# A linear-attention normalizer replicated over the partitions: TensorE matmuls exchanged for a round trip through DRAM

## Chip, cores and metric

The kernel runs on one core of a Trainium2 chip. The metric is the device time of one execution in microseconds; the time before is the median of three runs. A profile was taken of one further execution. Engines are named as in the profile: PE is TensorE (PEld its weight loads), DVE VectorE, ACT ScalarE, POOL GpSimd, SP SyncE, which issues most DMAs here.

## What is computed

A token block of 2048 x 640 is layer-normalized; one branch is a linear attention with 32 heads of width 20 and a learned feature map, the other a gated MLP of width 1536; their product is added to the input. Cut to what matters here:

```python
qkv = (xn @ wqkv)                            # q, k, v: 32 heads of width 20
pq, pk = q @ w_phi, k @ w_phi                # per head
phi_q = concat(softmax(pq), softmax(-pq))    # 40 features per head
phi_k = concat(softmax(pk), softmax(-pk))
kv  = einsum("bhsf,bhsd->bhfd", phi_k, v)
z   = einsum("bhsf->bhf", phi_k)             # the normalizer: 32 * 40 = 1280 numbers
num = einsum("bhqf,bhfd->bhqd", phi_q, kv)
den = einsum("bhqf,bhf->bhq", phi_q, z) + 1e-6
s   = (num / den) @ wo
g   = silu(gelu(xn @ w1 + b1) @ w2 + b2)
out = x + s * g
```

The change concerns `z` alone: 1280 numbers that must stand on all 128 partitions, because queries lie with one token on each partition and `den` is formed there by an elementwise product and sums.

## The kernel before

**Phase 1 (to about 249 us)** goes over 16 tiles of 128 tokens: keys, values and queries are projected on TensorE in three passes of split floats (`project`, L332), exponentials are formed, and key-value products are accumulated in one PSUM bank named `kv` (`kv_acc`, L403), two tiles of tokens in one go. A value tile carries a column of ones beside each head, so one row of each head's block of `kv` is the sum of its key features, which is `z`. Exponentials of the queries are stored to DRAM (`e_dram`). At the end of the phase `kv_rest` copies the bank to the SBUF tile `kvr` (128 x 360) by three ScalarE copies (L607): the normalizer then lies in four rows of `kvr`, on partitions 20, 52, 84 and 116, as pieces of 120 numbers (three heads each).

**Phase 2 (to about 535 us)** is the MLP, in 12 units: two halves of the tokens by 6 groups of 256 hidden columns. Its instructions are put out in the order written by hand. A unit runs, on TensorE, the seven parts of the hidden layer (`part`, L654, 54 matmuls of 512 columns, a scheme of sums and differences that saves products), then two down-projections (`down`, L683, 30 matmuls each). Around them:

- ScalarE applies Gelu (`act`, L659) and forms the high half of a hidden tile (L661), VectorE the low half (`act_lo`, L665). The tiles are named h11, h22, h21, h12 in the order of their making; the first down-projection uses h11 and h21, the second h12 and h22. VectorE collects the down-projections (L690 in the first group, L692 later).
- The next unit's `w1` forms are made on GpSimd (L419) and split by ScalarE (L430) and GpSimd (L431); `w2` is split by ScalarE (L146) and GpSimd (L148; VectorE in unit 0).
- SP's queue gets, in each unit and in this order, the raw weight loads of the next unit (L154), a block of normalized inputs (`xhi`, `xlo`, L703 and L704) and the exponentials of a block of queries (`eq`, L723).
- `q_norm` normalizes that block of queries: GpSimd multiplies it with the replicated normalizer (`ez<-eq,zrep`, L729), VectorE sums over heads, GpSimd scales (L371), and SP stores the result to `phi_dram` (L746).

In unit 0, between the last part of the hidden layer and the first down-projection, stands the call

```python
        if unit == 0:
            zf = kv_norm(kvr)
```

`kv_norm` makes the replicated normalizer `zrep` (128 x 1280, in one of 23 rotating slabs). Its first reader is `q_norm` of the query block that unit 1 treats; its last is near the end of the kernel. PSUM is a pool of eight banks (`bankB`) by then, given out in rotation.

**Phase 3 (from about 535 us)** forms the attention's numerators (L773, L784), projects with `wo` (L848), applies the gate and stores.

A pattern of the change is in the kernel already: `pair_stats` stores means and scales of two tiles to `st_dram` (L293) and loads them back broadcast over all partitions (L295).

The functions that the change touches, with the line numbers of the profile:

Of the kernel before, what the change touches and what calls it, by code (L numbers as in the profile page):

```python
# [8 lines left out]
F32 = mybir.dt.float32  # L9
F32R = mybir.dt.float32r  # L10
AF = mybir.ActivationFunctionType
# [3 lines left out]
S, D, H, DH, F = 2048, 640, 32, 20, 1536  # L15
P = 128
# [30 lines left out]
def hedgehog_gated_mlp_kernel(ctx: ExitStack, tc: tile.TileContext, x, xt_in, wqk, bd, wv, wo, w1, b1, w2, b2, out_t):  # L47
    nc = tc.nc
# [4 lines left out]
    dram = ctx.enter_context(tc.tile_pool(name="dram", bufs=1, space=bass.MemoryType.DRAM))  # L53
# [27 lines left out]
    def slab(dt, name, shape=(P, 2, D)):  # L81
        return slabs.tile(list(shape), dt, tag="S", name=name)
# [7 lines left out]
    def bankB(name="pB"):  # L90
        return pools["B"].tile([P, 512], F32, tag="B", name=name)
# [4 lines left out]
    xd_dram = dram.tile([P, 9, 2, CW], F32, name="xd_dram")  # L96
    w1_dram = dram.tile([NG, P, 2, 2048], F32, name="w1_dram")
    g_dram = dram.tile([KC, P, 2, CW], F32, name="g_dram")
    st_dram = dram.tile([NT // 2, 2, P, 2], F32, name="st_dram")

    ident = const.tile([P, P], F32, name="ident")
# [499 lines left out]
    def kv_rest():  # L601
        kv_pair(NT - 2)
        kvr = const.tile([P, 360], F32, name="kvr")
        nc.gpsimd.memset(kvr[64:96, 320:360], 0.0)
        nc.gpsimd.memset(kvr[96:, 240:360], 0.0)
        for p, a, b in ((P, 0, 240), (96, 240, 320), (64, 320, 360)):
            nc.scalar.activation(kvr[:p, a:b], kvp[0][:p, a:b], AF.Copy)  # L607
        return kvr


    def kv_state(kvr):
# [8 lines left out]
        for r in range(3):  # L620
            nc.vector.tensor_tensor(bdl[:80, 40 * r:40 * r + 40].rearrange("p (h d) -> p h d", d=20),
                                    ps[:80, None, 320:340].to_broadcast([80, 2, 20]),
                                    mask[:80, :2, None].to_broadcast([80, 2, 20]), op=OP.mult)
    def kv_norm(kvr):
        zf = slab(F32, "zrep")[:].rearrange("p a b -> p (a b)")
        for e, n in enumerate((360, 360, 320, 240)):
            ps = bankB()
            nc.tensor.matmul(ps[:, :n], ident[:, 32 * e + 20:32 * e + 21].to_broadcast([P, P]), kvr[:, :n],
                             start=True, stop=True)
            m = n // 120  # L630
            nc.scalar.activation(zf[:, :960].rearrange("p (g r) -> p g r", r=480)[:, :, 120 * e:120 * e + 120],
                                 ps[:, :240].rearrange("p (g r) -> p g r", r=120), AF.Copy)
            if n > 240:
                nc.scalar.activation(zf[:, 960 + 120 * e:720 + 120 * e + n], ps[:, 240:n], AF.Copy)
        return zf


# [220 lines left out]
    zf, none = None, iter(())  # L858
# [6 lines left out]
    kvr = kv_rest()  # L865
# [8 lines left out]
    for unit in range(units):  # L874
        h, g = divmod(unit, NG)
# [69 lines left out]
        if unit == 0:  # L945
            zf = kv_norm(kvr)
# [146 lines left out]
```

## Time and profile before

| | |
|---|---|
| median of three runs | 681.69 us (680.76, 681.69, 681.69) |
| the profiled execution | 680.42 us, of which the span of the instructions 678.7 us |
| PE busy | 673.7 us, 99% of the span |
| PEld busy | 591.3 us, 87% |
| DVE busy | 456.4 us, 67% |
| POOL busy | 382.1 us, 56% |
| ACT busy | 253.1 us, 37% |
| granted TensorE clock | full in all 40 slices |
| DMA | 125.42 MB, in the mean 185 GB/s |

The page gives busy shares over the span. A busy share is an average, and a matmul's recorded end is modelled; what an instruction costs is read from start to start in the timeline, and whether it matters from the chain that ended last and from the view of waits. A line number in the profile is that of the kernel before; a helper's line stands for all its calls.

### The profile page before, as it was taken

Reading aid. Unit: us, or ns where it says so; the run is one execution under the profiler, and the core shown is the slowest. Engines: PE = TensorE matmul, PEld = TensorE weight load, DVE = VectorE, ACT = ScalarE, POOL = GpSimd, SP = SyncE. Lnnn points to the kernel's source line nnn. Section 1 sums busy time; section 2 is a strip of 40 time slices with the busy share of each in tenths; the row PEclk is TensorE's granted clock in tenths of the full one; section 3 lists DMA queues with packets and bytes.
Section 4 is the critical chain, followed back from the end, with each engine's and each line's share of the span. In section 5 each row is a group of like instructions: output and inputs, shape, how many; then the busy total and the mean of one; then the engine's idle time right before and its main releaser. Section 6 shows DMA issues by size and latency. Waiting matters only on the chain.

```text
span 678.7 us, 11993 instructions
## 1 busy us (share of the span) xinstructions
PE 673.7 (99%) x4727; PEld 591.3 (87%) x4727; DVE 456.4 (67%) x729; ACT 253.1 (37%) x400; POOL 382.1 (56%) x351
## 2 busy tenths in 40 slices
PE   9999999999999999999999999999999999999998
PEld 9999999999999998888888888888888887777877
DVE  5786575887786456586988784586876665774232
ACT  3523213333223237244245238533133264425440
POOL 3653355757668275857878861716546640783221
PEclk9999999999999999999999999999999999999999
DMA  8820234543441433339678696477363491988433
GB/s 335 309 79 2 32 121 125 203 108 122 96 174 59 158 123 117 110 111 359 205 248 307 242 427 249 148 247 256 125 216 116 178 384 35 330 292 286 154 93 109
DMA packets 73966, 125.42 MB, mean 185 GB/s; under 512 B 5822, under 2 KB 42686, under 8 KB 73014
## 3 DMA queue, kind: packets, MB, share of 16 engines
q1 hardware_dynamic: 71606, 114.17, 49.0%
q10 hardware_dynamic: 2304, 10.49, 4.2%
q8 instruction: 37, 0.61, 0.4%
q14 instruction: 19, 0.16, 0.1%
HBM read 79.54 MB, written 45.10 MB: 184 GB/s over the span
## 4 chain that ended last, share of the span: by engine, by line
PE 93%; DMA 3%; DVE 2%; POOL 1%; issue 1%; SPq 0%; ACT 0%; DVEq 0%; POOLq 0%
PE pA L332 30%; PE pB L683 23%; PE pB L654 20%; PE pB L848 11%; PE pB L784 3%; PE kv L403 2%; PE pB L773 2%; DMA raw<-in_wo_dram 2%; DMA phi<-phi_dram 1%; PE pA L173 1%; POOL wv L148 1%; PE pA L470 1%; PE pA L318 1%; PE pB L791 1%; DVE st L197 0%
## 5 line engine op out<-in xcount | busy, mean ns | idle before, releaser
L683 PE MATMUL pB<-hs,w2s 128*128 128x512 f32 x720 | 167.1, 390 | 0.0
L683 PEld LDWEIGHTS pB<-hs,w2s 128*128 128x128 f32 x720 | 134.7, 188 | 29.3 <-PE pB L784 0.8
L654 PE MATMUL pB<-xp,w1s 128*128 128x512 f32 x324 | 81.3, 389 | 0.0
L654 PE MATMUL pB<-xd,w1s 128*128 128x512 f32 x324 | 79.3, 389 | 0.0
L358 ACT ACTIVATE e<-e 128x1280 f32<-128x1280 f32 x32 | 40.7, 1273 | 92.2 <-POOL e L353 91.8
L848 PE MATMUL pB<-oT,wo 128*128 128x512 f32 (+2 forms) x315 | 73.9, 386 | 0.0
L692 DVE TENSOR_TENSOR y<-pB,y 128x512 f32<-128x512 f32 x100 | 63.8, 679 | 12.3 <-PE pB L683 12.1
L654 PEld LDWEIGHTS pB<-xd,w1s 128*128 128x128 f32 x324 | 60.8, 188 | 12.6
L654 PEld LDWEIGHTS pB<-xp,w1s 128*128 128x128 f32 x324 | 60.7, 188 | 12.7 <-DVE pB L929 0.2
L848 PEld LDWEIGHTS pB<-oT,wo 128*128 128x128 f32 x315 | 57.1, 188 | 14.2 <-ACT ph L776 1.2
L371 POOL TENSOR_TENSOR eq<-eq,rc 128x1280 f32<-128x1280 f32 x16 | 37.9, 2370 | 50.8 <-DVE rc L742 50.8
L371 POOL TENSOR_TENSOR e<-e,rc 128x1280 f32<-128x1280 f32 x16 | 39.0, 2439 | 47.4 <-DVE rc L391 47.1
L353 POOL TENSOR_TENSOR e<-nr,e 128x640 f32<-128x640 f32 x32 | 45.5, 1424 | 29.9 <-DVE nr L352 26.6
L332 PE MATMUL pA<-wv,xp 128*128 128x320 f32 x384 | 60.5, 310 | 0.3 <-POOL wv L148 0.3
L659 ACT ACTIVATE pB<-pB,b1t 128x512 f32<-128x512 f32 x48 | 31.8, 662 | 75.7 <-PE pB L654 26.7
L332 PE MATMUL pA<-wk,xp 128*128 128x320 f32 x384 | 59.6, 310 | 0.0
L332 PE MATMUL pA<-wq,xp 128*128 128x320 f32 x384 | 58.8, 309 | 0.0
L332 PEld LDWEIGHTS pA<-wv,xp 128*128 128x128 f32 x384 | 57.0, 188 | 0.5 <-POOL wv L148 0.5
L332 PEld LDWEIGHTS pA<-wq,xp 128*128 128x128 f32 x384 | 56.9, 188 | 0.3 <-PE pA L332 0.3
L332 PEld LDWEIGHTS pA<-wk,xp 128*128 128x128 f32 x384 | 56.9, 188 | 0.0
L729 POOL TENSOR_TENSOR ez<-eq,zrep 128x1280 f32<-128x1280 f32 x16 | 47.3, 2958 | 0.4 <-PE pB L784 0.2
L431 POOL TENSOR_TENSOR w1s<-raw,w1s 128x640 fp32r<-128x640 f32 (+1 forms) x18 | 25.7, 1427 | 37.0 <-ACT w1s L430 29.9
(145 smaller groups left out, 1052.6 us busy)
## 6 DMA issues: line engine op xcount, KB each, us to landing
raw<-in_w_dram SPq DMA_DIRECT2D x42, 320.0 KB, 4.3
e_dram<-e ACTq DMA_DIRECT2D x16, 640.0 KB, 3.2
eq<-e_dram SPq DMA_DIRECT2D x16, 640.0 KB, 6.8
phi_dram<-eq SPq DMA_DIRECT2D x16, 640.0 KB, 3.5
phi<-phi_dram SPq DMA_DIRECT2D x16, 640.0 KB, 8.7
xt<-in_x_dram SPq DMA_DIRECT2D x16, 320.0 KB, 5.2
xres<-in_xt_dram SPq DMA_DIRECT2D x20, 256.0 KB, 4.2
out_dram<-xres SPq DMA_DIRECT2D x18, 256.0 KB, 3.0
```

The source lines that it names most:

```text
L332: nc.tensor.matmul(ps[:, hf, :HALF], stat_x(q, o, k, a), ws[k][:, b, hf * HALF:(hf + 1) * HALF], start=n == 0, stop=n == 3 * KC - 1)
L353: nc.gpsimd.tensor_tensor(e5[:, :, :, 1, :], nr[:, :, :, None].to_broadcast([P, 2, 16, DH]), e5[:, :, :, 0, :], op=OP.subtract)
L358: nc.scalar.activation(ef, ef, AF.Exp)
L371: nc.gpsimd.tensor_tensor(e3, e3, rc[:, :, None].to_broadcast([P, 64, DH]), op=OP.mult)
L431: nc.gpsimd.tensor_tensor(sl[:, 1, :n], src, sl[:, 0, :n].bitcast(F32), op=OP.subtract)
L654: nc.tensor.matmul(bank[ch][:], tl[:, a, off + wo_:off + wo_ + P], mov(blk, b), start=new and n == 0, stop=n == len(mms) - 1, skip_group_c ...
L659: nc.scalar.activation(ps, ps, AF.Gelu_apprx_tanh, bias=b1t[:, f:f + 1])
L683: nc.tensor.matmul(ps[:], ws[i][:, b, d * P:(d + 1) * P], hs[o][i][:, a, :], start=i == n == 0, stop=(i, n) == (GF - 1, 2), skip_group_che ...
L692: nc.vector.tensor_tensor(y, ps[:], y, op=OP.add)
L729: nc.gpsimd.tensor_tensor(zv, ef, zf, op=OP.mult)
L784: nc.tensor.matmul(po[64 * e:64 * e + 64, :256], bdk[:n, 2 * j + e, :], ph[:n, e * 256:(e + 1) * 256], start=True, stop=True)
L848: nc.tensor.matmul(ps[:, mv], w, o[:, mv], start=n == 0, stop=n == 15, skip_group_check=True)
```

## The change

In `kv_norm`, four matmuls go that each replicated one row of `kvr` over the partitions (a column of the identity matrix, repeated 128 times, as the weights), with four PSUM banks and the seven ScalarE copies that took the pieces to their places in `zrep`. In their stead five small DMAs store the pieces of the four rows in the right order to a DRAM tensor `z_dram`, and one DMA loads its first 1280 numbers to all 128 partitions. All six are issued by SP, at the same place in the order of the calls. `q_norm` and the rest are as before.

```diff
+    z_dram = dram.tile([1440], F32, name="z_dram")
...
     def kv_norm(kvr):
+        zv = z_dram.rearrange("(g e r) -> e g r", e=4, r=120)
+        for e, m in enumerate((3, 3, 2, 2)):
+            nc.sync.dma_start(zv[e:e + 1, :m], kvr[32 * e + 20:32 * e + 21, :120 * m].rearrange("p (g r) -> p g r", r=120))
+        nc.sync.dma_start(z_dram[1200:2 * D].unsqueeze(0), kvr[84:85, 240:320])
         zf = slab(F32, "zrep")[:].rearrange("p a b -> p (a b)")
-        for e, n in enumerate((360, 360, 320, 240)):
-            ps = bankB()
-            nc.tensor.matmul(ps[:, :n], ident[:, 32 * e + 20:32 * e + 21].to_broadcast([P, P]), kvr[:, :n],
-                             start=True, stop=True)
-            m = n // 120
-            nc.scalar.activation(zf[:, :960].rearrange("p (g r) -> p g r", r=480)[:, :, 120 * e:120 * e + 120],
-                                 ps[:, :240].rearrange("p (g r) -> p g r", r=120), AF.Copy)
-            if n > 240:
-                nc.scalar.activation(zf[:, 960 + 120 * e:720 + 120 * e + n], ps[:, 240:n], AF.Copy)
+        nc.sync.dma_start(zf, z_dram[:2 * D].partition_broadcast(P))
         return zf
```

In the built order of instructions TensorE has the four matmuls less, ScalarE the seven copies less, and SP the six DMAs more: after the load of the exponentials for unit 1 and before the raw weight loads for unit 2. VectorE and GpSimd have the same instructions in the same order.

## The prediction

> **What bounds the kernel now.** I read the page first, and in it the shares of the chain that ended last.
>
> ```profile
> PE 93%; DMA 3%; DVE 2%; POOL 1%; issue 1%; SPq 0%; ACT 0%; DVEq 0%; POOLq 0%
> ```
>
> TensorE (PE) carries 93% of the chain. Next I asked the view of waits for TensorE alone; this is all of it (engine and line that waited, who released it, us in total, times, longest):
>
> ```profile
> PE pA L470 <- PEq L1083: 0.8, 1, 0.8
> PE pA L332 <- POOL wv L148: 0.3, 1, 0.3
> PE pB L784 <- DVE oT L788: 0.3, 1, 0.3
> PE pA L318 <- DVE xt L213: 0.2, 1, 0.2
> ```
>
> TensorE waits 1.6 us in the whole run. So its instruction stream is the clock of this kernel: what is taken out of that stream shortens the run by its length, unless something then comes late. Third, the chain in order of time around the change (start, us, what):
>
> ```profile
> 261.29 2.15 PE pB L628 x8
> 263.45 13.63 PE pB L683 x60
> 277.08 12.24 PE pB L654 x54
> 289.32 13.60 PE pB L683 x60
> ```
>
> The four normalizer matmuls (L628; eight records) lie on the chain between unit 0's hidden-layer matmuls (L654) and its first down-projection (L683). In unit 1 L683 follows L654 with nothing between: what unit 0 will look like afterwards.
>
> **The change, part by part.**
>
> *TensorE's four matmuls go.* The timeline of TensorE alone (start, us, engine, line):
>
> ```profile
> 259.09 2.20 PE L654 MATMUL pB<-xp,w1s 128*128 128x512 f32 x9
> 261.13 2.31 PE L628 MATMUL pB<-kvr,ident 128*128 128x360 f32 x8
> 263.11 8.08 PE L683 MATMUL pB<-hs,w2s 128*128 128x512 f32 x34
> ```
>
> Three readings of their price: start to start, 263.11 − 261.13 = 1.98 us; the chain's piece, 2.15; the busy time with the modelled end of the last, 2.31. I take 1.98: ends are modelled, starts are recorded, and the neighbour before them also hands over from start to start (261.13 − 259.09 = 2.04 for nine matmuls). Ends for the range: 1.98 to 2.31, less what comes late instead.
>
> The Trainium skill, "TensorE: Matmul & The Clock Gate" (Part 1: The HAM clock gate), has back-to-back matmuls of N columns start N ÷ 2.4 GHz + about 2.5 ns apart. By that rule eight records of 320 columns in the mean would take some 1.1 us (an estimate from the page), the gain would be 1.1 us and the time 680.6; the starts above do not agree, at 248 ns each.
>
> *What is late next on TensorE.* The down-projection would begin at 261.13. It goes through nine matmuls on h11 and then to h21; one matmul takes 13.60/60 = 0.227 us by the chain's row. The halves of h11 and h21 come from ScalarE (ACT, the high half) and VectorE (DVE, the low half). Two timelines, of DVE and of ACT:
>
> ```profile
> 260.11 0.69 DVE L665 TENSOR_TENSOR hs<-pB,hs 128x512 fp32r<-128x512 f32 x1
> 261.29 0.69 DVE L665 TENSOR_TENSOR hs<-pB,hs 128x512 fp32r<-128x512 f32 x1 [0.49 <-ACT hs L661]
> 262.48 0.69 DVE L665 TENSOR_TENSOR hs<-pB,hs 128x512 fp32r<-128x512 f32 x1 [0.49 <-ACT hs L661]
> ```
>
> ```profile
> 261.85 0.60 ACT L661 ACTIVATE hs<-pB 128x512 fp32r<-128x512 f32 x1
> ...
> 264.50 0.60 ACT L661 ACTIVATE hs<-pB 128x512 fp32r<-128x512 f32 x1
> ...
> 266.41 0.81 ACT L430 ACTIVATE w1s<-raw 128x640 fp32r<-128x640 f32 x1
> ```
>
> The three DVE rows are the low halves of h11, h22 and h21. None of these instructions depends on the removed matmuls, so they keep their times. h11's low half is done at 260.80 and needed at the third matmul, 261.13 + 2 × 0.227 = 261.58. h21's high half is done at 262.45 and needed at the tenth, 263.17; its low half is done at 263.17 and needed at the twelfth, 263.63. The narrowest margin is 0.46 us. If it fails, TensorE loses what is missing, tenths at most. h12's high half ends at 265.10, its low half 0.69 later, for the second down-projection at 261.13 + 30 × 0.227 = 267.9. Accumulator banks: four fewer are drawn, so the down-projections take over banks from the hidden layer's parts, as they do in every later unit.
>
> *Seven ScalarE copies go* (L631, L634). They stand between 265.10 and the next unit's weight copies (L430) at 266.41, so L430 moves up by 1.31 us, and with it GpSimd's (POOL's) halves of those weights. ScalarE is not on the chain here: no gain of its own, but the weights of unit 1 keep pace with a TensorE that arrives 1.98 earlier, except for 0.67 us.
>
> *Six DMAs come on SP's queue*, after the load of query block 8 (L723) and ahead of the four weight loads for unit 2 (L154). SP's own timeline, and the ScalarE row that finishes `kvr`:
>
> ```profile
> 232.62 0.73 SPq L704 DMA_DIRECT2D xlo<-xp_dram  x1
> 233.46 1.84 SPq L723 DMA_DIRECT2D eq<-e_dram  x1
> 245.20 11.64 SPq L154 DMA_DIRECT2D raw<-in_w_dram  x4
> 269.63 0.53 SPq L703 DMA_DIRECT2D xhi<-xp_dram  x1
> ```
>
> ```profile
> 249.58 0.55 ACT L607 ACTIVATE kvr<-kv 128x240 f32<-128x240 f32 x3
> ```
>
> The kernel has the same pattern already: layer-norm statistics are stored to DRAM and loaded back broadcast over partitions. Its rows price the new one, with the longest of its own size beside them: the DMA issues (last column: median us to landing), and the issue itself on SP (ns, the least, median and most).
>
> ```profile
> eq<-e_dram SPq DMA_DIRECT2D x16, 640.0 KB, 6.8
> ...
> bc<-st_dram SPq DMA_DIRECT2D x4, 256.0 KB, 5.6
> ...
> st_dram<-pst SPq DMA_DIRECT2D x4, 2.0 KB, 2.8
> ```
>
> ```profile
> L293 SPq DMA_DIRECT2D st_dram<-pst x4: 359/360/367, 76.5 to 176.3; - x4
> ```
>
> `kvr` is complete at 250.13. Five stores at 0.36 are issued by 251.9; the last lands 2.8 later (a store of 2 KB) or at worst 6.8 (640 KB), 254.7 to 258.7; the spread, 640 KB, is issued in another 0.36 and lands 5.6 to 6.8 later: 260.7 to 265.9. I take the early end, since the stores hold 5 KB together. Its slab's last reader is the final query projection, long past. Who waits for it is GpSimd's first `ez` (L729):
>
> ```profile
> 276.87 2.96 POOL L729 TENSOR_TENSOR ez<-eq,zrep 128x1280 f32<-128x1280 f32 x1
> 279.79 3.10 POOL L148 TENSOR_TENSOR w2s<-raw,w2s 128x640 fp32r<-128x640 f32 x2
> 285.32 0.74 POOL L419 TENSOR_TENSOR st<-raw 128x256 f32<-128x256 f32 x1 [2.44 <-PE pB L654]
> ```
>
> Even 1.98 earlier, `ez` starts at 274.9, 9 us after the latest landing. Behind `ez` on GpSimd stand unit 1's `w2s` halves; the first is needed at the second matmul of unit 1's down-projection, 289.32 + 0.23 − 1.98 = 287.6, so `ez` may start as late as 287.6 − 1.55 − 2.96 = 283.1. Against that the spread has 17 us of cover or more.
>
> Queued behind the spread's wait are the four raw loads. The first, at 245.20 before, now goes out at 255.1 to 259.1; even with 6.8 to land it is there by 266, and its first user (L419) can start no earlier than 285.32 − 2.44 − 1.98 = 280.9. The next load after them (L703, 269.63, or 267.65 if it moves with TensorE) finds SP free: four issues at 0.36 end by 260.6. All six DMAs: nothing on the path.
>
> *Downstream.* TensorE waits only once after unit 0, 0.3 us at L784, and a chain of loads ends there:
>
> ```profile
> 534.57 0.70 DVE y L692
> ...
> 538.27 8.63 DMA phi<-phi_dram
> 546.92 10.80 DMA raw<-in_wo_dram
> ...
> 560.91 1.08 PE pB L784 x8
> ```
>
> That chain is set off by a VectorE addition that follows TensorE's own matmuls, so it starts 1.98 earlier too and still costs 0.3.
>
> **Sum.** −1.98 on TensorE, 0 elsewhere. The profiled execution took 680.42: 678.4 afterwards. The median of the runs shown is 1.27 above it, 681.69: 679.7 afterwards, a gain of 0.29%. About 0.2% (1.36 us) is what a measurement of this kernel can tell from no change.
>
> **The rivals.**
>
> *Handed back or smaller (within 0.2%).* If the loads before 560.91 ran on a clock of their own, TensorE's wait there would grow from 0.3 to 2.3 us and the time would stay at 681.7. For: 19 us of that stretch are DMA. Against: its first link is the row L692 above. Another way to the same place is a hole shorter than its starts say: 1.1 us gives 680.6. Against: the recorded starts.
>
> *The spread comes late (slower).* If the five stores landed one after another, each as slowly as a 640 KB load, the chain would be 250.13 + 5 × (0.36 + 6.8) + 0.36 + 6.8 = 293.1; `ez`, `w2s` and unit 1's down-projection would be 10.0 late, the net 8.0, the time 689.7. It turns the sign beyond a landing at 283.1 + 1.98 = 285.1. For: two transfers in series through DRAM, with very short rows. Against: SP issued L723 0.84 us after L704 began, well before a 640 KB load lands, so stores to different places needn't wait for each other; and the pattern's own rows are 2.8 and 5.6.
>
> In that case alone, by the Trainium skill, "TensorE: Matmul & The Clock Gate" (Part 1: The HAM clock gate), an idle window of some 3.4 us halves the clock until some 3.4 us of work have passed, up to 1.7 us more (an estimate from the page); no run here shows it, since TensorE is never idle that long.
>
> *The change doesn't do what it says* has little room: in the built order of instructions the three blocks named above are the only difference on any engine.
>
> **How the numbers follow.** Forecast 679.7, chance 0.85; its own range goes from the fastest run shown less the largest price, 680.42 − 2.31 = 678.1, to the slowest less 1.5 (the 0.46 margin failing), 680.2. Handed back or smaller, 0.10: 680.6 to 681.7. Spread late, 0.05: beyond 683. The range is 678.1 to 681.0: the forecast's own, and as far into the second case as its smaller-hole version with a little scatter. Faster by over 0.2%: 0.82 (the forecast, less 0.03 for scatter); within: 0.13; slower: 0.05.
>
> **What would show it.** Right: L683 of unit 0 starts within 2.1 us of the last L654 group; chain pieces after it are as long as before and 2 us earlier; the spread lands near 262 and no `ez` waits for it; TensorE's waits stay at four small rows. Wrong: a wait of L683 for L665 or L661 in unit 0, a wait of `ez` for the spread, or more than 0.3 us at L784.

## The result, and the profile after

The changed kernel takes 678.81 us in the median of seven runs (678.44 to 680.23), the kernel before 681.16 in the median of seven (680.76 to 681.69): a ratio of 0.9968, with a 95% interval of 0.9957 to 0.9980. That is 2.35 us, 0.34%: clear of scatter, and over the 0.2% that the prediction set, at which the interval ends.

The chain in order of time, around the change (start, us, what), after one row of the kernel before that the prediction does not show; in the changed kernel L651 is the hidden layer (L654 before) and L680 the down-projection (L683 before):

```profile
249.03 12.26 PE pB L654 x54
```

```profile
249.25 12.27 PE pB L651 x54
261.51 13.60 PE pB L680 x60
275.11 12.24 PE pB L651 x54
287.35 13.60 PE pB L680 x60
```

The 2.15 us piece is gone, and unit 0 looks like unit 1. From unit 0's first hidden-layer matmul to unit 1's first down-projection it is 287.35 − 249.25 = 38.10 us; before it was 289.32 − 249.03 = 40.29. So 2.19 us went. TensorE's own timeline shows the new neighbours:

```profile
259.31 2.20 PE L651 MATMUL pB<-xp,w1s 128*128 128x512 f32 x9
261.35 13.76 PE L680 MATMUL pB<-hs,w2s 128*128 128x512 f32 x60
```

The first L680 starts 2.04 us after the last group of L651, as nine matmuls need. The view of waits for TensorE's matmuls, whole; a wait for h11 or h21, where the margin was 0.46 us, does not appear:

```profile
PE pA L471 <- PEq L1080: 0.8, 1, 0.8
PE pA L333 <- POOL wv L149: 0.3, 1, 0.3
PE pA L174 <- DMA folds<-in_wqk_dram: 0.2, 1, 0.2
```

This view, here and in the prediction, counts the waits of matmuls alone. A wait of a weight load (PEld) is not in it: in the changed kernel one of 0.5 us for L926 in unit 4, of which more below.

SP's timeline has the six DMAs (four stores in one row, the fifth, then the spread) and what was queued behind them; the row below it is the spread's time from issue to landing:

```profile
250.38 2.76 SPq L628 DMA_DIRECT2D z_dram<-kvr  x4
253.19 0.42 SPq L629 DMA_DIRECT2D z_dram<-kvr  x1
255.40 0.35 SPq L631 DMA_DIRECT2D zrep<-z_dram  x1
255.79 1.84 SPq L155 DMA_DIRECT2D raw<-in_w_dram  x4
267.66 0.58 SPq L700 DMA_DIRECT2D xhi<-xp_dram  x1
```

```profile
zrep<-z_dram SPq DMA_DIRECT2D x1, 640.0 KB, 4.7
```

The spread is in place at about 260.1. GpSimd comes for it 15 us later and does not wait:

```profile
275.61 2.95 POOL L726 TENSOR_TENSOR ez<-eq,zrep 128x1280 f32<-128x1280 f32 x1
```

The raw loads go out at 255.8, behind the spread as foreseen, and SP is idle again ten us before the next load.

### The profile page after: what moved, and what is told of

The parts are those of the page before. It is cut to its first block, busy times and chain, and to the rows that moved or that the text cites. A ratio compares the mean times of both kernels' runs of the same rounds, so it can differ in the third digit from the quotient of the medians.

```text
span 677.1 us, 11973 instructions
## 1 busy us (share of the span) xinstructions
PE 672.1 (99%) x4719; PEld 589.8 (87%) x4719; DVE 458.1 (68%) x729; ACT 252.1 (37%) x393; POOL 381.3 (56%) x351
## 4 chain that ended last, share of the span: by engine, by line
PE 92%; DVE 3%; DMA 3%; POOL 1%; issue 1%; ACT 0%; SPq 0%; DVEq 0%; ACTq 0%; POOLq 0%
PE pA L333 30%; PE pB L680 22%; PE pB L651 20%; PE pB L845 11%; PE pB L781 3%; PE pB L770 2%; PE kv L404 2%; DMA raw<-in_wv_dram 1%; PE pA L174 1%; DMA folds<-in_wqk_dram 1%; DVE y L689 1%; DMA xt<-in_x_dram 1%; PE pB L788 1%; DVE xhi L705 0%; POOL wv L149 0%
## 5 line engine op out<-in xcount | busy, mean ns | idle before, releaser
L680 PE MATMUL pB<-hs,w2s 128*128 128x512 f32 x720 | 167.0, 390 | 0.0
L680 PEld LDWEIGHTS pB<-hs,w2s 128*128 128x128 f32 x720 | 134.6, 188 | 29.4 <-PE pB L781 0.8
L651 PE MATMUL pB<-xp,w1s 128*128 128x512 f32 x324 | 81.4, 390 | 0.1
L651 PE MATMUL pB<-xd,w1s 128*128 128x512 f32 x324 | 79.3, 389 | 0.0
L651 PEld LDWEIGHTS pB<-xp,w1s 128*128 128x128 f32 x324 | 60.7, 188 | 13.1 <-DVE pB L926 0.5
L651 PEld LDWEIGHTS pB<-xd,w1s 128*128 128x128 f32 x324 | 60.8, 188 | 12.6
L372 POOL TENSOR_TENSOR eq<-eq,rc 128x1280 f32<-128x1280 f32 x16 | 37.9, 2369 | 50.6 <-DVE rc L739 49.2
L372 POOL TENSOR_TENSOR e<-e,rc 128x1280 f32<-128x1280 f32 x16 | 39.0, 2439 | 47.6 <-DVE rc L392 47.4
L432 POOL TENSOR_TENSOR w1s<-raw,w1s 128x640 fp32r<-128x640 f32 (+1 forms) x18 | 25.7, 1426 | 35.5 <-ACT w1s L431 28.4
```

Of the source, the lines that this page charges most:

```text
L372: nc.gpsimd.tensor_tensor(e3, e3, rc[:, :, None].to_broadcast([P, 64, DH]), op=OP.mult)
L432: nc.gpsimd.tensor_tensor(sl[:, 1, :n], src, sl[:, 0, :n].bitcast(F32), op=OP.subtract)
L651: nc.tensor.matmul(bank[ch][:], tl[:, a, off + wo_:off + wo_ + P], mov(blk, b), start=new and n == 0, stop=n == len(mms) - 1, skip_group_c ...
L680: nc.tensor.matmul(ps[:], ws[i][:, b, d * P:(d + 1) * P], hs[o][i][:, a, :], start=i == n == 0, stop=(i, n) == (GF - 1, 2), skip_group_che ...
```

## The experiments

The theory: what is taken out of TensorE's stream is the gain, and the path through DRAM costs nothing because GpSimd needs the result long after. The rivals: a part of the gain belongs to the seven ScalarE copies; the path through DRAM is close to deciding; and, seen in the first comparison of the traces, a wait of TensorE for VectorE in unit 4 (0.4 us) that the change might have brought and that eats a part of the gain. Four kernels ran together on one chip, four more on another; each group has its own runs of the kernel before.

**The changed kernel again.**

> The changed kernel again, on the same chip as the three others of this group, so that they can be compared with it and not only with the kernel before. Both theories: 2.0 to 2.4 us under the kernel before; in the profile the first L680 follows the last L651 of unit 0 after 2.04 us, and TensorE waits about 0.4 us for L926 in unit 4.

Measured: 679.05 us against 681.36 for the kernel before, a ratio of 0.9968 (0.9955 to 0.9980). The first comparison repeats.

**The four matmuls put back, unread.**

```diff
         nc.sync.dma_start(zf, z_dram[:2 * D].partition_broadcast(P))
+        for e, n in enumerate((360, 360, 320, 240)):
+            ps = bankB()
+            nc.tensor.matmul(ps[:, :n], ident[:, 32 * (e % 4) + 20:32 * (e % 4) + 21].to_broadcast([P, P]), kvr[:, :n],
+                             start=True, stop=True)
```

> The changed kernel with the four replicating matmuls put back into TensorE's stream at their old place; nobody reads their banks, zrep still comes by DMA, and no ScalarE copy comes back. If the gain is the length of TensorE's stream (theory), all of it goes: the time of the kernel before within 0.4 us, and unit 0 to the end of unit 1's hidden layer longer by 2.0 (the price by starts) to 2.2 us (by the chain) than in the changed kernel. If the seven copies on ScalarE had a share (rival), that share stays: with an even split the time lies 1 us under the kernel before.

Measured: 681.27 us, a ratio to the kernel before of 0.9998 (0.9989 to 1.0007). The whole gain is gone, though neither the copies nor the old way of `zrep` came back. The chain of this run (L655 hidden layer, L634 the matmuls put back, L684 down-projection):

```profile
249.98 12.26 PE pB L655 x54
262.25 2.15 PE pB L634 x8
264.40 13.63 PE pB L684 x60
278.04 12.24 PE pB L655 x54
290.28 9.75 PE pB L684 x43
```

290.28 − 249.98 = 40.30, the 40.29 of the kernel before.

**The same matmuls twice**, eight in all: the loop above runs over the four widths two times.

> The changed kernel with the four replicating matmuls put in twice, unread (eight in all). It prices one set. Theory that a set costs 2.19 us (what the two profiles and the run with one set show): from unit 0's first L651 to unit 1's first L680 42.5 us, against 38.1 without and 40.3 with one set, and the time 2.2 us over the kernel before. Rival, the prediction's price by starts of 1.98: 42.1 us.

```profile
249.65 12.26 PE pB L655 x54
261.91 4.31 PE pB L634 x16
266.22 13.63 PE pB L684 x60
279.85 12.24 PE pB L655 x54
292.09 12.92 PE pB L684 x57
```

Measured: 683.54 us, 1.0034 of the kernel before (1.0022 to 1.0045), and 292.09 − 249.65 = 42.44. With none, one and two sets the stretch is 38.10, 40.30 and 42.44 us and the time 679.0, 681.3 and 683.5: 2.17 us a set in the trace, 2.2 to 2.3 in the times. The second set costs what the first does, and starts told too little. (683.5 is from the second chip, where the kernel before took 681.32.)

**Seven ScalarE copies put back**, no matmul.

```diff
+    scr = const.tile([P, 240], F32, name="scr")
...
         nc.sync.dma_start(zf, z_dram[:2 * D].partition_broadcast(P))
+        for n in (240, 120, 240, 120, 240, 80, 240):
+            nc.scalar.activation(scr[:, :n], kvr[:, :n], AF.Copy)
```

> The changed kernel with seven ScalarE copies of the old widths put in at their old place, from kvr to a scratch tile that nobody reads; no matmul comes back. Theory: the same as the changed kernel within 0.3 us, since the weights of unit 1 have several us to spare; L431 of unit 1 moves back by about 1.3 us and TensorE waits no more than before. Rival (the copies had a share): slower than the changed kernel by about 1 us.

Measured: 679.15 us, the ratio to the kernel before 0.9968 (0.9957 to 0.9980), the same as the changed kernel. ScalarE's timeline in this run (L634 the copies, L432 the first weight copy of unit 1):

```profile
264.62 2.68 ACT L634 ACTIVATE scr<-kvr 128x240 f32<-128x240 f32 x7
267.21 0.72 ACT L432 ACTIVATE w1s<-raw 128x640 fp32r<-128x640 f32 x1
```

The copies move the weights back by over 2 us, more than the 1.3 expected, and TensorE does not wait for those weights. The copies had no share.

**The spread made late.** Five or fourteen more copies in series on SP's queue, from DRAM to DRAM, ahead of the spread:

```diff
+    zb = [dram.tile([1440], F32, name=f"zb{i}") for i in range(5)]    # 14 in the other run
...
+        src = z_dram
+        for i in range(5):                   # 14 in the other run
+            nc.sync.dma_start(zb[i][:2 * D].unsqueeze(0), src[:2 * D].unsqueeze(0))
+            src = zb[i]
-        nc.sync.dma_start(zf, z_dram[:2 * D].partition_broadcast(P))
+        nc.sync.dma_start(zf, src[:2 * D].partition_broadcast(P))
```

> The changed kernel with five more copies in series on SP's queue, DRAM to DRAM, each waiting for the one before, between the stores of the normalizer and its spread; the four raw loads behind them are late with it. At 2.2 us (this pattern's own store, from the changed kernel's profile) to 3.2 us a copy the spread is issued at 266 to 271 and lands at 271 to 276, ahead of the 283 at which GpSimd's first ez must start. Theory (cover of 17 us or more): the time of the changed kernel within 0.4 us, no wait on TensorE. Rival (the path through DRAM is on the critical chain as soon as it grows): 11 to 16 us slower than the changed kernel.

Measured: 678.93 us, 0.9965 of the kernel before (0.9952 to 0.9978): eleven us more of DRAM path cost nothing. SP and GpSimd in this run:

```profile
257.98 6.94 SPq L634 DMA_DIRECT2D zb<-zb  x4
266.43 0.35 SPq L636 DMA_DIRECT2D zrep<-zb  x1
```

```profile
275.83 2.96 POOL L731 TENSOR_TENSOR ez<-eq,zrep 128x1280 f32<-128x1280 f32 x1
```

> The same with fourteen copies in series: the spread is issued at 286 to 300 and lands at 291 to 305. Theory: beyond 283 each us is lost one for one behind ez and w2s, so 8 to 22 us on TensorE's way to unit 1's down-projection, in the profile a wait of L680 for GpSimd's w2s; a part can come back, since unit 1 and 2 have slack of their own on the other engines but none on TensorE. So 8 to 22 us slower than the changed kernel. Rival: the raw loads behind the copies set the limit instead; then the wait shows in unit 2 at the hidden layer's weights.

Measured: 687.42 us, 1.0088 of the kernel before (1.0073 to 1.0103), 8.5 us over the run with five copies. That lies in the expected 8 to 22 by luck: a copy took 2.0 us, the spread landed before the expected 291 to 305, and by the rule of one us lost for each us after 283 only 5.6 us would have gone. The DMA issues and the view of waits:

```profile
zrep<-zb SPq DMA_DIRECT2D x1, 640.0 KB, 4.5
...
zb<-zb SPq DMA_DIRECT2D x13, 5.0 KB, 2.0
```

```profile
PE pB L685 <- POOL w2s L150: 6.3, 1, 6.3
```

The spread was issued at 284.15 and landed at 288.65; `ez` started at 288.72, 5.6 us after the 283.1 at which the prediction let it start at the latest. The wait is where the prediction put it, at unit 1's second down-projection matmul for `w2s`. TensorE's timeline around it:

```profile
287.61 0.39 PE L685 MATMUL pB<-hs,w2s 128*128 128x512 f32 x1
294.33 16.37 PE L685 MATMUL pB<-hs,w2s 128*128 128x512 f32 x59 [6.33 <-POOL w2s L150]
310.54 1.52 PE L656 MATMUL pB<-xp,w1s 128*128 128x512 f32 x6
```

Without a wait the second matmul would start 0.23 us after the first, so it is 6.5 us late (the view's 6.3 counts from the modelled end of the first). That is more than the 5.6 of `ez`, mainly because the first half of `w2s` took 2.7 us (291.57 to 294.28) and not 1.55; a VectorE instruction (L716) ran beside it from 291.53 to 292.89. The profile's chain goes through a raw load that landed at 290.31, but `w2s` began as `ez` ended, at 291.60, so the load did not decide.

A further 2.8 us is TensorE's clock: the 59 matmuls after the wait took 310.54 − 294.33 = 16.21 us from start to start, where at 13.60 for 60 they take 13.37. The busy time by windows shows it (the granted clock is the figure before the last two):

```profile
287.00:294.00 7.00, 1.00 (x5) 0.49 (x3) 3.31 (x5) 3.70 (x6) 5.28 (x2) 0.95 1.02 337
294.00:298.00 4.00, 3.67 (x9) 2.90 (x10) 0.00 (x0) 0.63 (x1) 3.92 (x6) 0.50 1.09 368
298.00:302.00 4.00, 4.00 (x15) 3.16 (x14) 2.57 (x3) 0.63 (x1) 4.00 (x4) 0.74 0.63 189
302.00:306.00 4.00, 4.00 (x19) 3.31 (x18) 3.90 (x9) 1.78 (x3) 2.65 (x3) 1.00 0.00 0
```

Together 6.5 + 2.8 = 9.3 us are lost. The two profiled executions differ by as much, 687.94 − 678.59 = 9.35; the medians by 8.5.

**The wait in unit 4.** The chain of the changed kernel has, in unit 4, a turn through VectorE that the first profile of before lacks (L926 is an addition of the hidden layer, L929 before):

```profile
362.23 0.71 DVE pB L926
362.94 0.04 issue
362.98 2.36 PE pB L651 x9
365.35 6.81 PE pB L680 x30
```

VectorE is behind with the additions, and TensorE's last part waits for a bank. From unit 3's first down-projection (339.08, 12.24 after the hidden layer's start in the chain) to unit 4's it is 26.27 us, 25.89 before. One experiment takes VectorE's load away from that place, one profiles the kernel before again.

```diff
         p1 = part(w1g, bank, 1)
-        next(q1, None)
+        if unit != 4:
+            next(q1, None)
...
         h12 = act(c12, f1)
+        if unit == 4:
+            next(q1, None)
```

> The changed kernel, but in unit 4 VectorE's sum and reciprocal of q_norm (L367 and L729, 2.0 us together) stand after the hidden layer's additions instead of ahead of them. If the wait of TensorE for L926 in unit 4 (0.5 us by the view of waits, 0.4 by the chain) is what keeps the gain below the price of the hole, that wait is gone and the run is 0.3 to 0.4 us under the changed kernel. If instead the wait only moves on (VectorE is as late at the next additions), a wait of the same size shows in the first down-projection of unit 4 or in unit 5 and the time stays.

Measured: 679.18 us, against 679.05 for the changed kernel beside it. In the trace the wait is gone, and unit 4's hidden layer takes the undisturbed 12.24 us:

```profile
353.22 12.24 PE pB L651 x54
365.46 6.57 PE pB L680 x29
```

The time did not follow; in this run 0.3 us of waiting at L781 were back, which the changed kernel lacks in two profiles, and the run with seven copies has. 0.4 us is less than the times of this group can settle (678.5 to 679.71 for the changed kernel alone).

> The kernel before, for a second profile. Both theories agree on unit 0: 40.3 us from the first L654 to unit 1's first L683. Open is the wait of TensorE for VectorE in unit 4, which cost 0.05 us in the first profile of before and 0.4 in three runs with the spread by DMA: if it belongs to the change it is again under 0.1 here; if it scatters from run to run it may be 0.4 here too. The start of unit 0 tells what the first phase scatters by, 249.0 in the first profile.

```profile
364.70 0.71 DVE pB L929
365.40 0.04 issue
365.45 2.33 PE pB L654 x9
367.78 2.27 PE pB L683 x10
```

Measured: 681.09 us, one run. The second profile of before has the wait as well: unit 3's first down-projection starts at 315.65 + 13.65 + 12.24 = 341.54, unit 4's at 367.78, 26.24 us apart. So the wait is not the change's; it comes and goes with the run (25.89 and 26.24 in two profiles of the same kernel). The rival falls.

What tells the runs apart stands in unit 3: GpSimd's scaling of a block of queries (L371, L372 after) and VectorE's addition of the two halves of the inputs (L708, L705 after). First the kernel before, then the changed one:

```profile
353.65 2.37 POOL L371 TENSOR_TENSOR eq<-eq,rc 128x1280 f32<-128x1280 f32 x1 [0.16 <-DVE rc L742]
354.70 2.67 DVE L708 TENSOR_TENSOR xhi<-xhi,xlo 128x1280 f32<-128x1280 f32 x1
```

```profile
352.11 2.36 POOL L372 TENSOR_TENSOR eq<-eq,rc 128x1280 f32<-128x1280 f32 x1
352.37 3.44 DVE L705 TENSOR_TENSOR xhi<-xhi,xlo 128x1280 f32<-128x1280 f32 x1
```

The two overlap by 1.32 us and the addition takes 2.67; they overlap by 2.10 and it takes 3.44. In the second profile of before it is 2.10 and 3.45. In units 1 to 3 of all ten profiles the addition takes 1.33 to 1.35 us and the overlap on top, while the scaling keeps to 2.36 to 2.38: the addition behaves as if it stood still as long as the scaling runs. The overlap in unit 3 is 1.3 in the first profile of before and with fourteen copies, and there unit 4 loses nothing (25.89 and 25.84 us); it is 2.1 in the other eight, and of these seven have the wait (26.24 to 26.36 us), all but the one in which VectorE's load was moved. Why GpSimd begins 1.05 us ahead of the addition in one run and 0.26 in another stays open, and no run moves the scaling alone.

No version here beats the changed kernel by more than scatter.

## Why the prediction was right

*The hole.* Right in kind: TensorE's stream set the time, and the run got shorter by what was taken out. The term that was mis-sized is the price, 1.98 us by starts: between equal landmarks it is 2.19, one set put back 2.20, a second 2.14. The chain's own piece (2.15) was the better reading. The start record there came ahead of the work: before, the first down-projection matmul is recorded at 263.11 and unit 1's first matmul at 276.92, 13.81 us later, after the change 274.95 − 261.35 = 13.60. The missing 0.21 us belongs to the removed matmuls. Where it may lie, the weight loads show: before, the first load of the down-projection is recorded at 263.08, 0.03 us ahead of its matmul, after the change at 261.13, 0.22 ahead. Behind the replicating matmuls the load was not done beforehand; that this makes the 0.21 was not tested. A price of 2.17 us for 1280 columns is 1.70 ns a column, where the down-projection takes 0.44 (0.227 us for 512). The profile shows the hidden layer's tiles written as fp32r and `kvr` as f32, and two records for each of the four matmuls; no run here varies the type.

*The rule of the Trainium skill on matmul spacing* ("TensorE: Matmul & The Clock Gate", Part 1: The HAM clock gate), by which the prediction estimated a hole of 1.1 us, does not hold for these matmuls: with one and two sets it is 2.2 and 4.3 us. The measurement that opens that part is of bf16 matmuls, and these multiply float32.

*What would come late instead:* nothing, as worked out. The margin of 0.46 us on h21 held. One reading was wrong without consequence: h12's low half did not follow its high half by 0.69 us before, it stood behind a VectorE copy that waited for TensorE and began at 266.85; after the change it begins at 265.36, ahead of the 267.9 that the prediction needed.

*The ScalarE copies* off the path: shown by the run that puts seven back.

*The DMAs.* The pattern's rows were good bounds: the last store was in by about 255.4 (254.7 to 258.7 foreseen), the spread landed at 260.1, just under 260.7 to 265.9, since its 640 KB took 4.7 us and not 5.6 or more. Stores came dearer to issue, 0.42 to 0.81 us each and not 0.36, and cheaper to land, about 2.2 us for the last and not 2.8. The cover stood: `ez` started at 275.6. With fourteen copies it started at 288.7, 5.6 us after the 283.1 that the prediction gave as the last moment, and TensorE was 6.5 us late.

*Downstream* the shift was handed on to the end. Between the two profiles, 1.6 us apart, the parts are: unit 0 begins 0.22 later, the hole gives 2.19, unit 4's wait takes 0.4, and the 0.3 at L784 falls away. That makes 1.9; small pieces elsewhere take back 0.3. The first and third of these parts scatter from run to run, and the fourth may: the run with seven copies and the one with the moved sum have the 0.3 again.

*The number.* 679.7 was the median of the first three runs, 681.69, less 1.98. The median of seven is 681.16: 0.53 of the 0.9 us that the forecast lay high come from there, 0.21 from the price, and the rest, under 0.2, is within scatter. That the range held did not need luck: the trace's 2.19 lies inside the prices of 1.98 to 2.31.

*The slower rival* did not come, and its mechanism exists: with fourteen copies in series it costs 8.5 us. The prediction's estimate of what the clock would add, up to 1.7 us, was too small; it measured 2.8.

## What to carry to other kernels

Where one engine never waits, price an edit by that engine's stream alone, and read the price from the chain's pieces or from two equal landmarks on either side, not from the start of the next instruction. Look at the waits of the weight loads too. A copy over partitions that is needed 25 us after its source could go through DRAM here: count its landing, find the last moment at which its first reader may start, and compare. Before a new wait in one trace is laid to the change, profile the kernel before a second time.

## What was not expected of the hardware

After TensorE had stood for 6.3 us it ran on at a granted clock of 0.50 for 4 us and 0.74 in the mean over the next 4, and lost 2.8 us more. The Trainium skill, "TensorE: Matmul & The Clock Gate" (Part 1: The HAM clock gate), has the clock halved after an idle window of about 3.4 us, until a window of about 3.4 us was busy, and says that these windows run free of what the kernel does. The halving is seen here. In narrower stretches the granted clock is 0.76 from 293.0 to 293.5, 0.50 up to 300.0 and 0.91 to 300.5, so it was halved from about 293.3 to 300.1: 5.3 us after TensorE fell idle, and for 6.8 us, of which TensorE worked 5.8. That is about two windows of 3.4 us. Nothing of it shows in the kernels before and after, whose TensorE never waits for a whole us.

VectorE's addition of two 128x1280 tiles (L705, L708 before) took 1.48 us with no GpSimd instruction beside it (unit 0 of the two runs with matmuls put back), and up to 3.45 beside GpSimd's scaling, which lost nothing by it. In unit 0, beside GpSimd's splitting of weights (L431), it was the other way too: the addition took 1.75 us before and 2.44 after the change, and the last of these splits 2.26 us, where it takes 1.02 in the first of those two runs.
